# A second piece of w_out behind the experts' weights, converted in the hand-over

## The chip, the cores and the metric

The kernel runs on one core of one Trainium2 chip. The metric is the device time of one launch in microseconds (us). The engines are called PE (TensorE, matrix products), ACT (ScalarE), DVE (VectorE), POOL (GpSimd) and SP (SyncE, which here only issues transfers). SBUF is the core's working memory, PSUM the memory that PE writes to.

## The reference

Three layers follow one another on 3072 tokens of 512 features: attention in chunks with eight memory keys, a soft mixture of eight experts, and a layer with a gated normalisation. All is float32.

```python
# 1: for each chunk c of 32 queries
k_full = np.concatenate([mem_k, k_ctx], axis=2)
scores = scale * np.matmul(q_c, k_full.transpose(0, 1, 3, 2))
a = softmax(scores)
out[:, :, c_start:c_end] = np.matmul(a, v_full)
...
# 2: x is the attention's output, one row per token
logits = x @ phi
slot_input = softmax(logits, over tokens).T @ x
for e in range(E):
    h = np.maximum(slot_input[e] @ w1[e], 0.0)
    slot_out[e] = h @ w2[e]
x = softmax(logits, over slots) @ slot_out
...
# 3
h = x @ w_in
e = np.exp(h - h_max)
sm = e / (np.sum(e, axis=-1, keepdims=True) + 1e-09)
solu = h * sm
mu = np.mean(solu, axis=-1, keepdims=True)
var = np.mean((solu - mu) ** 2, axis=-1, keepdims=True)
ln = (solu - mu) / np.sqrt(var + 1e-06) * g_ln
return (ln @ w_out).astype(np.float32)
```

w_in (512x1024) and w_out (1024x512) belong to layer 3. They arrive as 64-bit words, which the kernel turns into float32 by itself; the experts' w1 and w2 arrive as float32.

## The kernel before

The program is one stream of instructions per engine, in the order in which the code is written (a manual schedule). It has four stages.

**Attention**, 0 to about 115 us: 32 steps g, each for two heads and 384 tokens. Per step SP issues the loads of keys, queries and values (`load_qk`, `load_v`) and, as the list LOADS says, one chunk of weights or none (`load_e`).

**Experts**, about 125 to 179 us: `units` lists 32 units in order, w1 or w2 of one expert and one half. Each needs two chunks of 128x1024 float32, 512 KB. Beside them run the softmax over slots (`combine`, with operations on POOL) and the conversion of w_out (`lane`).

**Hand-over**, about 179 to 197 us: the list TAIL names the steps in the order in which they are written out. `so` copies the experts' result (L491) and turns it (L495, L496); `min` multiplies it by w_in (L502) and copies the product m out in two halves (L506, L507). `ha`, `hb`, `max`, `e`, `u`, `y0`, `y1` are the first token tile's product (L595), maximum (L601), exponential (L604), product with its sum (L610) and mean taken off (L624, L628). `s0`, `t0`, `w0`, `s1`, `t1`, `w1` prepare m for the tiles behind (L514, L517, L521); `keep` is ten matmuls whose result nobody reads (L483). `yt0`, `yt1` transpose the tile on PE (L652); `hi0`, `hi1` copy that from PSUM to yh (L673, ACT), and `lo0`, `lo1` take the remainder yl (L677, DVE).

**Main stage**, to the end: 24 token tiles, each with 24 matmuls of 128x512 (L683): for each of eight pieces f of w_out, yh by whi[f], yh by wlo[f] and yl by whi[f]. `final` sorts the steps of all tiles by planned times. For tile 0 eighteen of the 24 matmuls (all of yh for pieces 0 to 6, yl for 0 to 3) stand on PE ahead of the product h(3) of tile 3 (L595), which takes the PSUM buffer that u of tile 1 (L610) has read; piece 7 of tile 0 stands behind it.

**A piece of w_out** is 128x512, one chunk of 512 KB as it arrives. Its conversion (`cast_ops`, then `wout_ops`) is a list of seven steps: two casts on ACT (L537, L538); an integer operation on DVE (L541); two more (L546, L549); the low part's product (L552) and its sum (L555), on the engine given as `eng`; whi, on ACT, with the piece's column of g as scale (L572); wlo, the remainder, on DVE (L576). w_in goes through the same `cast_ops` with its low part on POOL. In the experts' stage pieces 0 to 6 are converted on ACT and DVE. Piece 7 is converted in the hand-over: the seven steps `l` of TAIL, called `last`.

**The queue of weights.** `chunks` is the order of loading: the eight chunks of w_in and seven of w_out in turn, the 64 of the experts, then piece 7. w_in and the experts take slots from the list `free`; a piece of w_out has a slot of its own, `wslot[j]`. The slot of piece 7 is in `free` too at the start, so that it serves one experts' chunk first (`release` does not give it back). A load waits on SP for what last read its slot.

Of the kernel before, what the change touches and what calls it, by code (L numbers as in the profile page):

```python
# [7 lines left out]
FP32 = mybir.dt.float32  # L8
# [4 lines left out]
ACTF = mybir.ActivationFunctionType  # L13
ALU = mybir.AluOpType
# [42 lines left out]
TAIL = (  # L57
    "so open l l l min l l e12 ha hb max s0 s1 t0 e keep w0 u t1 y0 y1 l w1 yt0 hi0 yt1 hi1 lo0 l lo1 e3"
).split()
# [4 lines left out]
LAG = 2  # L64

CLATE = 3
TORD = [1, 0]
# [11 lines left out]
def tile_kernel(ctx: ExitStack, tc: tile.TileContext, kr, vr, w1, w2, w_in, w_out, cst, out):  # L79
# [37 lines left out]
    def at(name, off, n, dt=FP32):  # L117
        o, size, tl = arenas[name]
        assert off + n <= size, (name, off, n, size)
        v = tl[:, o + off:o + off + n]  # L120
        return v if dt == FP32 else v.bitcast(dt)
# [41 lines left out]
    wslot = [at(f"w{j}", 0, 1024) for j in range(FC)]  # L163
    free.append(wslot[-1])
    whi, wlo = {}, {}
# [32 lines left out]
    units += [("w2", E - 1, 0), ("w2", E - 1, 1)]  # L198
    chunks = [(w, j) for j in range(2 * KC) for w in ("win", "wout")][:-1]
    for u in units:  # L200
        chunks += [u[:2] + (2 * u[2] + j,) for j in range(2)]
    chunks.append(("wout", FC - 1))
    slot_of = {}
# [25 lines left out]
    def release(key):  # L229
        if slot_of[key] is not wslot[-1]:  # L230
            free.append(slot_of[key])
# [332 lines left out]

    def wout_ops(j, t):

        w = wo[t % len(wo)]

        def hi():
            area(f"w{j}", [(f"wh{j}", DM), (f"wl{j}", DM)])  # L570
            whi[j], wlo[j] = at(f"wh{j}", 0, DM, FP32R), at(f"wl{j}", 0, DM, FP32R)
            act.activation(out=whi[j], in_=w, func=ACTF.Copy, scale=g_sb[:, j:j + 1])  # L572

        return cast_ops(slot_of["wout", j], at("tmp", 512 * (t % 2), 512), w, dve) + [
            hi,
            lambda: dve.scalar_tensor_tensor(  # L576
                out=wlo[j], in0=w, scalar=g_sb[:, j:j + 1], in1=whi[j].bitcast(FP32), op0=ALU.mult, op1=ALU.subtract
            ),
        ]
# [178 lines left out]
    with tc.manual_schedule():  # L758
# [107 lines left out]
        begun = 0  # L866
        waiting = [lambda t, j=j: wout_ops(j, t) for j in range(FC - 1)]
        for n, u in enumerate(units):
# [33 lines left out]
        def e3():  # L902
# [3 lines left out]

        bufs = {}
        last = wout_ops(FC - 1, 1)
        calls = dict(
            so=m_so, open=open_final, min=m_in, l=lambda: last.pop(0)(),  # L910
        )
# [86 lines left out]
```

## Time and profile before

| | |
|---|---|
| time of the runs, median of 3 | 339.71 us (339.42 to 341.79) |
| span of the profiled execution | 340.1 us |
| busy: PE, DVE, ACT, POOL | 308.3, 248.5, 240.6, 194.3 us |
| chain that ended last, by engine | PE 57%, DMA 21%, DVE 9%, ACT 7%, POOL 3% |
| costliest group | L683 on PE, 552 matmuls, 130.5 us busy |

The profile is of one execution, and its span is compared with the median above. Times in the timelines are microseconds from the span's start. An instruction's row gives its start, its length, and in brackets how long its engine had been idle before it and for what. PE's lengths overlap, as matmuls are pipelined. The chain of waits is followed back from the last instruction, each link to what released it.

### The profile page before, as it was taken

What the parts mean: (1) busy time and instruction counts of PE and PEld (TensorE: products, weight loads), DVE (VectorE), ACT (ScalarE), POOL (GpSimd) and SP (SyncE); (2) the same over time, 40 slices, a digit from 0 to 9 for tenths busy, and PEclk for the clock granted to TensorE, in tenths of its full rate; (3) what the DMA queues carried; (4) which work ended last, traced back from release to release, by engine and by line L of the source; (5) the groups of instructions that cost most, each with busy time, mean ns of one, the idle gap of its engine ahead of it and who ended that gap; (6) DMA issues with size and microseconds to landing.
All of it is one profiled execution on the core that took longest, in us unless ns stands there. A gap on an engine that the chain in (4) does not pass through costs nothing.

```text
span 340.1 us, 8121 instructions
## 1 busy us (share of the span) xinstructions
PE 308.3 (91%) x2964; PEld 214.4 (63%) x2964; DVE 248.5 (73%) x445; ACT 240.6 (71%) x453; POOL 194.3 (57%) x381
## 2 busy tenths in 40 slices
PE   2987797898997989888989999999999999999996
PEld 1765565666665443323324778888888888888885
DVE  4787987998898338999105895887887878878540
ACT  2777958869886537685414787988888888888631
POOL 6668987797899023132100347777766667576600
PEclk9999999999999999999999999999999999999999
DMA  7999999999999999999990003566676666766621
GB/s 284 413 414 414 414 409 415 324 384 387 319 377 413 411 418 418 409 413 416 421 359 3 0 34 134 208 216 239 230 235 223 217 218 217 247 202 226 224 93 63
DMA packets 38919, 97.41 MB, mean 286 GB/s; under 512 B 4320, under 2 KB 14944, under 8 KB 38880
## 3 DMA queue, kind: packets, MB, share of 16 engines
q1 hardware_dynamic: 38736, 96.68, 75.3%
q8 instruction: 23, 0.38, 0.4%
q10 hardware_dynamic: 144, 0.22, 0.2%
q14 instruction: 16, 0.13, 0.1%
HBM read 80.11 MB, written 16.78 MB: 285 GB/s over the span
## 4 chain that ended last, share of the span: by engine, by line
PE 57%; DMA 21%; DVE 9%; ACT 7%; POOL 3%; issue 2%; SPq 0%; ACTq 0%; DVEq 0%; POOLq 0%
PE bank L683 36%; DMA e_area<-in_w_dram 9%; DMA kq_area<-in_kr_dram 7%; DMA ex_area<-in_w_dram 6%; PE h L595 3%; PE bank L303 3%; PE bank L365 2%; POOL v_area L291 2%; PE bank L243 1%; PE bank L322 1%; PE bank L314 1%; ACT s_area L275 1%; PE bank L280 1%; PE bank L328 1%; ACT s_area L317 1%
## 5 line engine op out<-in xcount | busy, mean ns | idle before, releaser
L683 PE MATMUL bank<-wh_area,yh_area 128*128 128x512 f32 x552 | 130.5, 391 | 0.0
L683 PEld LDWEIGHTS bank<-wh_area,yh_area 128*128 128x128 f32 x552 | 103.4, 188 | 22.5
L291 POOL TENSOR_SCALAR v_area<-v_area 64x780 f32<-64x780 f32 x64 | 57.0, 890 | 15.7 <-DMA v_area<-in_vr_dram 5.3
L243 PE MATMUL bank<-kq_area 128*32 128x128 f32 x768 | 29.2, 288 | 9.4 <-ACT kq_area L287 7.4
L666 DVE STREAM_TRANSPOSE yq_area<-yq_area 128x1024 f32<-128x1024 f32 x20 | 24.9, 1245 | 16.7 <-DMA yq_area<-z 16.7
L303 PE MATMUL bank<-v_area,s_area 128*32 128x130 f32 x768 | 27.9, 276 | 10.1 <-ACT s_area L283 5.7
L610 DVE SCALAR_TENSOR_TENSOR eb_area<-h,eb_area 128x1024 f32<-128x1024 f32 x24 | 29.2, 1218 | 10.5 <-ACT eb_area L604 10.1
L648 POOL TENSOR_SCALAR cst_area<-cst_area 128x1 f32<-128x1 f32 x72 | 26.8, 372 | 7.7
L243 PEld LDWEIGHTS bank<-kq_area 128*32 128x32 f32 x768 | 20.2, 114 | 15.4 <-ACT kq_area L287 9.9
L303 PEld LDWEIGHTS bank<-v_area,s_area 128*32 128x32 f32 x768 | 19.9, 108 | 15.7 <-ACT s_area L283 5.3
L601 DVE TENSOR_REDUCE cst_area<-h 128x1 f32<-128x1024 f32 x24 | 29.0, 1216 | 0.9 <-PE h L595 0.9
L637 POOL TENSOR_SCALAR cst_area<-cst_area 128x1 f32<-128x1 f32 x24 | 13.9, 579 | 25.7 <-ACT eb_area L604 23.8
L287 ACT COPY kq_area<-kq_area 64x512 f32<-64x512 f32 x39 | 23.8, 611 | 6.5 <-DMA kq_area<-in_kr_dram 6.4
L604 ACT ACTIVATE eb_area<-h,cst_area 128x1024 f32<-128x1024 f32 x24 | 26.7, 1111 | 1.9 <-DVE cst_area L601 1.9
L633 ACT ACTIVATE eb_area<-eb_area,cst_area 128x1024 f32<-128x1024 f32 x24 | 27.3, 1139 | 0.1
L630 ACT ACTIVATE eb_area<-eb_area,cst_area 128x1024 f32<-128x1024 f32 x20 | 23.1, 1155 | 5.2 <-DVE eb_area L610 4.9
L677 DVE TENSOR_TENSOR yh_area<-yq_area,yh_area 128x1024 fp32r<-128x1024 f32 x20 | 24.6, 1228 | 2.3 <-ACT yh_area L673 2.3
L673 ACT CAST yh_area<-yq_area 128x1024 fp32r<-128x1024 f32 x20 | 21.0, 1049 | 6.3 <-DVE yq_area L666 6.3
L649 POOL TENSOR_SCALAR cst_area<-cst_area 128x1 f32<-128x1 f32 x72 | 21.2, 295 | 7.1
L701 ACT ACTIVATE eb_area<-bank,cst_area 128x512 f32<-128x512 f32 x23 | 15.8, 686 | 9.2 <-POOL cst_area L639 6.9
L261 DVE TENSOR_REDUCE cst_area<-bank 128x6 f32<-128x384 f32 x32 | 17.6, 551 | 6.0 <-PE bank L243 5.9
L317 ACT COPY s_area<-bank 128x384 f32<-128x384 f32 x32 | 15.4, 483 | 7.9 <-PE bank L314 7.7
(150 smaller groups left out, 571.8 us busy)
## 6 DMA issues: line engine op xcount, KB each, us to landing
e_area<-in_w_dram SPq DMA_DIRECT2D x41, 512.0 KB, 10.1
kq_area<-in_kr_dram SPq DMA_DIRECT2D x32, 448.0 KB, 6.4
v_area<-in_vr_dram SPq DMA_DIRECT2D x32, 390.0 KB, 6.8
ex_area<-in_w_dram SPq DMA_DIRECT2D x22, 512.0 KB, 9.9
z<-eb_area SPq DMA_DIRECT2D x20, 512.0 KB, 2.8
yq_area<-z SPq DMA_DIRECT2D x80, 128.0 KB, 2.9
out_dram<-eb_area SPq DMA_DIRECT2D x23, 256.0 KB, 2.1
e_area<-in_w_in_dram SPq DMA_DIRECT2D x8, 512.0 KB, 8.1
```

The lines of the kernel that those rows point to most:

```text
L243: pe.matmul(out=bk[32 * j:32 * j + 32, t * 128:(t + 1) * 128], lhsT=kq[i][:, KS + c * CH:KS + (c + 1) * CH], rhs=kwin(g % 2, c), start=Tru ...
L287: act.copy(out=o, in_=i)
L291: pool.tensor_scalar(out=o, in0=i, scalar1=1.0, scalar2=0.0, op0=ALU.mult, op1=ALU.add)
L303: pe.matmul(out=bk[32 * j:32 * j + 32, t * 2 * VW:(t + 1) * 2 * VW], lhsT=atb[g % 2][:, c * CH:(c + 1) * CH], rhs=vz[g % 2][:, :, c * VW:( ...
L601: dve.tensor_reduce(out=sc("nm", i), in_=fin["h"][i % 2], axis=AX.X, op=ALU.max, negate=True)
L604: act.activation(out=eb[i % FIN], in_=fin["h"][i % 2], func=ACTF.Exp, bias=sc("nm", i), accum_out=sc("s", i))
L610: dve.scalar_tensor_tensor(out=ub[i % FIN], in0=fin["h"][i % 2], scalar=-1.0 / FF, in1=eb[i % FIN], op0=ALU.mult, op1=ALU.mult, accum_out= ...
L633: act.activation(out=sq, in_=ub[i % FIN], func=ACTF.Square, scale=-float(FF), bias=sc("nu", i), accum_out=sc("vs", i))
L648: pool.tensor_scalar(out=t, in0=r, scalar1=r, scalar2=xx, op0=ALU.mult, op1=ALU.mult)
L666: dve.transpose(out=yv[i % FIN].rearrange("p (f a t) -> p a f t", f=FC, a=4), in_=yq[i % FIN].rearrange("p (a f t) -> p a f t", f=FC, a=4),)
L677: dve.tensor_tensor(out=yl[i % FIN][:, sl], in0=tps(i, sl) if i < NPE else yv[i % FIN], in1=yh[i % FIN][:, sl].bitcast(FP32), op=ALU.subtract,
L683: pe.matmul(out=fin["o"][i % 2], lhsT=a[i % FIN][:, f * 128:(f + 1) * 128], rhs=w[f], start=start, stop=stop)
```

## The change

NOUT, new, is the number of pieces of w_out that are loaded ahead of the experts' weights: six instead of seven. Pieces 6 and 7 are loaded behind them, and both their slots serve an experts' chunk first. Piece 6 is no longer converted in the experts' stage: TAIL has seven new steps `p`, called `side`, that convert it in the hand-over, with its low part on POOL. Its last two steps differ from the other pieces': g is multiplied into it on POOL, ACT copies whi from that, and POOL takes wlo. Piece 7's low part moves from DVE to POOL, and its step for whi moves from ahead of `w1` to behind `hi1`. The scratch of piece 6 is the area `acc`.

```diff
 TAIL = (
-    "so open l l l min l l e12 ha hb max s0 s1 t0 e keep w0 u t1 y0 y1 l w1 yt0 hi0 yt1 hi1 lo0 l lo1 e3"
+    "so open p l p p l l min p p l l e12 ha hb max s0 s1 t0 e keep w0 u t1 y0 y1 w1 yt0 hi0 yt1 hi1 p p l lo0 l lo1 e3"
 ).split()
...
+NOUT = FC - 2
...
-    free.append(wslot[-1])
+    free += wslot[NOUT:]
...
-    chunks = [(w, j) for j in range(2 * KC) for w in ("win", "wout")][:-1]
+    chunks = [(w, j) for j in range(2 * KC) for w in ("win", "wout") if w == "win" or j < NOUT]
...
-    chunks.append(("wout", FC - 1))
+    chunks += [("wout", j) for j in range(NOUT, FC)]
...
-        if slot_of[key] is not wslot[-1]:
+        if not any(slot_of[key] is w for w in wslot[NOUT:]):
             free.append(slot_of[key])
...
-    def wout_ops(j, t):
+    def wout_ops(j, t, t2=None, eng=dve, last=None):
...
+        t2 = at("tmp", 512 * (t % 2), 512) if t2 is None else t2
+        last = last or dve
...
-            act.activation(out=whi[j], in_=w, func=ACTF.Copy, scale=g_sb[:, j:j + 1])
-
-        return cast_ops(slot_of["wout", j], at("tmp", 512 * (t % 2), 512), w, dve) + [
+            if last is pool:
+                pool.tensor_scalar(out=w, in0=w, scalar1=g_sb[:, j:j + 1], scalar2=None, op0=ALU.mult)
+                act.copy(out=whi[j], in_=w)
+            else:
+                act.activation(out=whi[j], in_=w, func=ACTF.Copy, scale=g_sb[:, j:j + 1])
+
+        if last is pool:
+            return cast_ops(slot_of["wout", j], t2, w, eng) + [
+                hi, lambda: pool.tensor_tensor(out=wlo[j], in0=w, in1=whi[j].bitcast(FP32), op=ALU.subtract),
+            ]
+        return cast_ops(slot_of["wout", j], t2, w, eng) + [
             hi,
             lambda: dve.scalar_tensor_tensor(
...
-        waiting = [lambda t, j=j: wout_ops(j, t) for j in range(FC - 1)]
+        waiting = [lambda t, j=j: wout_ops(j, t) for j in range(NOUT)]
...
-        last = wout_ops(FC - 1, 1)
+        last = wout_ops(FC - 1, 1, eng=pool)
+        side = wout_ops(FC - 2, 0, t2=acc, eng=pool, last=pool)
         calls = dict(
-            so=m_so, open=open_final, min=m_in, l=lambda: last.pop(0)(),
+            so=m_so, open=open_final, min=m_in, l=lambda: last.pop(0)(), p=lambda: side.pop(0)(),
         )
```

Line numbers behind `wout_ops` are 11 to 12 higher after the change, those ahead of it 1 higher.

On DVE, in the hand-over from the first conversion to the maximum of tile 0 and w0. First before; w7_area is piece 7 as it arrived, wo2_area its float32 form, cst_area holds scratch and small values, h0 is tile 0's product in PSUM, bank0 a PSUM bank.

```order
L541 TENSOR_SCALAR wo2_area_1800<-wo2_area_1800 128x512
L546 SCALAR_TENSOR_TENSOR wo2_area_1800<-w7_area_83,wo2_area_1800 128x512
L549 TENSOR_SCALAR cst_area_66<-wo2_area_1800 128x512
L552 TENSOR_TENSOR cst_area_66<-w7_area_83,cst_area_66 128x512
L555 TENSOR_TENSOR wo2_area_1800<-wo2_area_1800,cst_area_66 128x512
L601 TENSOR_REDUCE cst_area_66<-h0_2242 128x1
L521 SCALAR_TENSOR_TENSOR m4_area_2223<-cst_area_66,bank0_84 128x512
```

The same place after the change; w6_area is piece 6.

```order
L542 TENSOR_SCALAR wo2_area_1800<-wo2_area_1800 128x512
L547 SCALAR_TENSOR_TENSOR wo2_area_1800<-w6_area_82,wo2_area_1800 128x512
L550 TENSOR_SCALAR cst_area_66<-wo2_area_1800 128x512
L542 TENSOR_SCALAR wo2_area_1800<-wo2_area_1800 128x512
L547 SCALAR_TENSOR_TENSOR wo2_area_1800<-w7_area_83,wo2_area_1800 128x512
L550 TENSOR_SCALAR cst_area_66<-wo2_area_1800 128x512
L612 TENSOR_REDUCE cst_area_66<-h0_2232 128x1
L522 SCALAR_TENSOR_TENSOR m4_area_2213<-cst_area_66,bank0_84 128x512
```

The low part of piece 7 has left DVE, and piece 6's three integer operations stand ahead of piece 7's.

On POOL, after the change, behind the last operation of `combine` (hr_area) and ahead of tile 0's variance (the operations on one column).

```order
L433 TENSOR_TENSOR hr_area_1801<-cst_area_66,hr_area_1801 128x6x64
L553 TENSOR_TENSOR cst_area_66<-w6_area_82,cst_area_66 128x512
L556 TENSOR_TENSOR wo2_area_1800<-wo2_area_1800,cst_area_66 128x512
L553 TENSOR_TENSOR cst_area_66<-w7_area_83,cst_area_66 128x512
L556 TENSOR_TENSOR wo2_area_1800<-wo2_area_1800,cst_area_66 128x512
L576 TENSOR_SCALAR wo2_area_1800<-wo2_area_1800,cst_area_66 128x512
L583 TENSOR_TENSOR wh6_area_2293<-wo2_area_1800,wh6_area_2293 128x512
L648 TENSOR_SCALAR cst_area_66<-cst_area_66 128x1
```

All six operations on 128x512 are new there; before, the first operation on one column (L637) followed `combine` directly.

On ACT, from t1 to the square of tile 0 (the last row). First before; h1 is the second PSUM buffer of the tiles' product, t and bank1 hold the transposed tile, wh7_area is whi[7].

```order
L517 CAST cst_area_66<-h1_2243 128x512
L628 ACTIVATE eb_area_2262<-eb_area_2262,cst_area_66 128x4x4x32
L572 ACTIVATE wh7_area_2285<-wo2_area_1800,cst_area_66 128x512
L673 CAST yh_area_2261<-bank1_85 128x512
L673 CAST yh_area_2261<-t_2241 128x512
L633 ACTIVATE eb_area_2262,cst_area_66<-eb_area_2262,cst_area_66 128x1024
```

The same place after.

```order
L518 CAST cst_area_66<-h1_2233 128x512
L639 ACTIVATE eb_area_2259<-eb_area_2259,cst_area_66 128x4x4x32
L684 CAST yh_area_2258<-bank1_85 128x512
L684 CAST yh_area_2258<-t_2231 128x512
L577 CAST wh6_area_2293<-wo2_area_1800 128x512
L579 ACTIVATE wh7_area_2297<-wo2_area_1800,cst_area_66 128x512
L644 ACTIVATE eb_area_2259,cst_area_66<-eb_area_2259,cst_area_66 128x1024
```

whi[7] has moved behind the two casts to yh, and whi[6] stands ahead of it. On DVE the rows behind are unchanged in order: yl, wlo[7], yl, and the maxima of tiles 1 and 2.

## Rows read from the trace of the kernel before

**Rows 1.** The chain of waits, 130 to 230 us: start, length, engine and line.

```profile
165.62 10.12 DMA e_area<-in_w_dram
175.78 1.05 PE bank L475 x4
...
195.23 1.24 DVE eb_area L610 x2
...
217.12 5.49 PE bank L683 x24
```

**Rows 2.** The stages table: busy time by engine, PE's granted clock, DMA share, GB/s.

```profile
160.00:175.00 15.00, 14.19 (x88) 4.31 (x82) 2.61 (x10) 6.07 (x16) 1.52 (x2) 1.00 1.03 418
```

**Rows 3.** The timeline of ACT in the hand-over: start, length, instruction, idle time before it.

```profile
179.93 0.68 ACT L537 ACTIVATE wo_area<-w_area 128x512 f32<-128x512 f32 x1
180.50 0.65 ACT L538 ACTIVATE w_area<-w_area 128x512 f32<-128x512 uint32 x1
182.48 0.59 ACT L506 COPY hr_area<-bank 128x512 f32<-128x512 f32 x1 [1.32 <-PE bank L502]
...
189.64 0.71 ACT L572 ACTIVATE wh_area<-wo_area,cst_area 128x512 fp32r<-128x512 f32 x1
190.26 0.58 ACT L673 CAST yh_area<-bank 128x512 fp32r<-128x512 f32 x1
190.73 0.59 ACT L673 CAST yh_area<-t 128x512 fp32r<-128x512 f32 x1
191.21 1.17 ACT L633 ACTIVATE eb_area<-eb_area,cst_area 128x1024 f32<-128x1024 f32 x1
```

**Rows 4.** The timeline of DVE in the hand-over.

```profile
181.15 0.42 DVE L541 TENSOR_SCALAR wo_area<-wo_area 128x512 int32<-128x512 int32 x1
181.60 0.69 DVE L546 SCALAR_TENSOR_TENSOR wo_area<-w_area,wo_area 128x512 int32<-128x512 int32 x1
182.33 0.43 DVE L549 TENSOR_SCALAR cst_area<-wo_area 128x512 int32<-128x512 int32 x1
...
185.16 1.23 DVE L601 TENSOR_REDUCE cst_area<-h 128x1 f32<-128x1024 f32 x1 [0.89 <-PE h L595]
...
190.87 0.69 DVE L677 TENSOR_TENSOR yh_area<-bank,yh_area 128x512 fp32r<-128x512 f32 x1 [0.71 <-ACT yh_area L673]
191.48 0.74 DVE L576 SCALAR_TENSOR_TENSOR wh_area<-wo_area,cst_area,wh_area 128x512 fp32r<-128x512 f32 x1
...
192.74 2.35 DVE L601 TENSOR_REDUCE cst_area<-h 128x1 f32<-128x1024 f32 x2
```

**Rows 5.** The timeline of PE in the hand-over.

```profile
189.56 0.66 PE L652 MATMUL bank<-cst_area,eb_area 128*128 128x128 f32 x4 [0.38 <-DVE eb_area L624]
...
191.41 4.29 PE L683 MATMUL bank<-wh_area,yh_area 128*128 128x512 f32 x18
196.51 0.73 PE L595 MATMUL h<-m_area,c4t_area 128*128 128x512 f32 x2 [0.81 <-DVE eb_area L610]
```

**Rows 6.** The load of w_out's piece 7: its issue, and how long until it landed.

```profile
169.35 0.33 SPq L225 DMA_DIRECT2D w_area<-in_w_out_dram  x1
...
DMA to landing us min/median/max: 10.2/10.2/10.2
```

**Rows 7.** POOL's groups for w_in's low parts: count, busy us, mean ns, idle before.

```profile
L552 POOL TENSOR_TENSOR cst_area<-e_area,cst_area 128x512 f32<-128x512 f32 x8 | 10.6, 1320 | 0.7
L555 POOL TENSOR_TENSOR cst_area<-cst_area 128x512 f32<-128x512 f32 x8 | 10.3, 1289 | 0.7
```

**Rows 8.** Timelines of POOL and DVE, two moments at which both work on SBUF.

```profile
98.84 1.86 POOL L291 TENSOR_SCALAR v_area<-v_area 64x780 f32<-64x780 f32 x2
100.02 0.95 DVE L541 TENSOR_SCALAR cst_area<-cst_area 128x512 int32<-128x512 int32 x1
...
146.37 1.01 POOL L432 TENSOR_TENSOR hr_area<-cst_area,hr_area 128x384 fp32r<-128x384 f32 x1 [3.67 <-ACT hr_area L428]
146.48 1.44 DVE L546 SCALAR_TENSOR_TENSOR wo_area<-w_area,wo_area 128x512 int32<-128x512 int32 x1
```

## Prediction

> **What bounds the kernel now.** I read the chain of waits first, then the stages table for the stretch where the chain is made of transfers, then the timelines of ScalarE (ACT), VectorE (DVE) and TensorE (PE) in the hand-over, and last the grouped rows of GpSimd (POOL).
>
> The chain [rows 1] shows three stretches around the change. From about 126 us until 175.74 it is one transfer of experts' weights behind another; the last such hop is shown, and PE's work on that chunk starts 0.04 us after the landing. (It is the third-last chunk; the last two land 1.25 us apart under the work that follows.) Then comes the hand-over, 175.8 to 196.5 us: short links of PE, ACT and DVE, none of them long. Behind 196.5 us the chain is PE alone, main matmuls (L683) to the end. So a microsecond saved or lost anywhere in the first two stretches arrives at the end of the program, as long as nothing beside the chain catches up.
>
> In the stages table [rows 2] the DMA engines are full from 160 to 175 us (share 1.03) at 418 GB/s. A chunk is 512 KB, 524,288 bytes, so one chunk takes 524288 / 418e3 = 1.25 us. That is the price of one place in the queue. In the same stretch PE, which waits for each chunk, shows a granted clock of 1.00, the 2.4 GHz level.
>
> In the hand-over every microsecond has an owner. ACT [rows 3] converts w_out piece 7 (L537, L538) between the copies of the slots' result and those of m_in, and makes whi[7] (L572) at 189.64, ahead of the two yh casts, which start at 190.26 and 190.73. That L572 is hidden: yh's first half could not start earlier, since the four transposes before it end at 189.56 + 0.66 = 190.22 [rows 5]. DVE [rows 4] converts piece 7 from 181.15 on (three integer operations, then the two of the low part), then has 0.89 us of idle time before max(0) at 185.16; later it runs yl, wlo[7] (191.48), yl, max(1) and max(2) (192.74) without a gap. PE sits idle 0.81 us [rows 5] for DVE's L610 at 195.23, the u of tile 1. DVE is therefore what sets the start of the main stage.
>
> **What the change does to the queue.** Piece 6 of w_out leaves the places in front of the experts' weights and goes behind them; its slot takes an experts' chunk instead, once. The attention loads and the number of chunks issued between them stay. Before, the last experts' chunk is the 79th of the weights' chunks (8 w_in, 7 w_out, 64 experts'); after, the 78th. The ring is one slot longer, so every place in the queue waits for the same release as before: the first chunk in the extra area is the 33rd place in both, the first one in a reused slot the 44th in both. The queue has work without a gap over this stretch, so the last experts' chunk lands one place earlier: **-1.25 us** [rows 2].
>
> The two pieces behind it are not late. Piece 7 was issued at 169.35 and landed 10.2 us later, at 179.55 [rows 6], three places behind the chunk of 175.74 (175.74 + 3 x 1.25 = 179.5); its place does not move, and piece 6 comes one place ahead of it, at about 178.3. ACT asks for piece 6 at 179.93 - 1.25 = 178.68 and for piece 7 two operations later (0.57 apart, [rows 3]) at 179.82. The cover is 0.3 us for either.
>
> **What the change does to the hand-over.** All times from here are on the clock of before; the shift of -1.25 us is added at the end.
>
> ACT: four conversions instead of two, 179.93 + 4 x 0.57 = 182.2, the last ending near 182.3. The copy of m_in's first half starts at 182.48 [rows 3], for PE. Hidden, by 0.2 us. ACT also loses the conversions of piece 6 in the experts' stage, and DVE its six operations there; that stage waits for transfers, so I count nothing.
>
> DVE before max(0): six operations (the integer parts of pieces 6 and 7) instead of five. The lengths of a triple are 0.42, 0.69 and 0.43 [rows 4]. Alone, the second triple would run 182.7 to 184.3, and max(0) would not notice. But now POOL works beside it: the four low-part operations, 1.32 and 1.29 us each [rows 7], the first as soon as piece 6's triple ends at 182.76.
>
> Here the trace has a warning [rows 8]. L546, 0.69 us at 181.60, took 1.44 us when it was issued at 146.48 behind a POOL operation that ran 146.37 to 147.38; it ended 0.54 us behind POOL. L541, 0.42 us at 181.15, took 0.95 at 100.02, with two POOL operations from 98.84 to 100.70; it ended 0.27 us behind them. So these DVE operations, which read and write only SBUF, stand still until POOL's has ended, and then need their length less about 0.15. Working this through: the first operation of piece 7 gets in before POOL (182.7 to 183.1); POOL's first holds until about 184.2; the DVE operation issued at 183.13 ends at 184.2 + 0.54 = 184.74; POOL's second, queued behind it, holds until about 185.85; DVE's last, short one ends at about 185.85 + 0.27 = 186.12, and max(0) starts at 186.05 instead of 185.16: **+0.9 us**. Bounds: 0, if they do not meet, since the idle 0.89 us covers the rest; 1.3, if POOL takes its second turn before DVE gets one (both DVE operations then follow 185.5: 0.54 + 0.43, max(0) near 186.45). I take 0.9, as in rows 8 DVE was let in when a POOL operation ended.
>
> The Trainium skill, page "SBUF — State Buffer", section "Who interferes with whom", has the same meeting as an exclusive lock: the second to issue blocks fully until the first is done. Read literally, DVE's whole length would follow POOL's end, 0.69 rather than 0.54, which over three blocked operations adds some 0.45 us to my sum below, 341.3 us in place of 340.8. The 0.54 us behind POOL in [rows 8] speaks for the shorter form.
>
> POOL itself is not late: its third and fourth operation end near 188.8, the multiplication by g at 190.1 at most (at the price of a two-input one, 1.32), and ACT wants it at 192.1 (below).
>
> DVE before max(1): whi[7] now stands on ACT behind both yh casts and the new cast whi[6]. ACT issues these 0.48 apart [rows 3], so whi[6] takes the place of L633 at 191.21 and whi[7] runs 191.69 to 192.40 (0.71). DVE's wlo[7], which stands between the two yl, ran at 191.48; it now starts at 192.43: **+0.95 us**. The second yl, max(1), max(2) and u(1) stand behind it on DVE, and PE's h(3) behind u(1). Nothing on DVE hides this, as there was no gap after 190.87. L633 and its variance on POOL move back by 1.0 to 1.5 us too; tile 0 needs its scale only when its matmuls are done, several us later.
>
> POOL's last new operation, wlo[6], starts when whi[6] is done, 0.6 us before wlo[7] is issued on DVE (0.48, and 0.12 that whi[7] is longer). It holds 1.3 us. wlo[7] has two SBUF inputs, so it stands 0.7 us and then needs some 0.57 instead of 0.74: **+0.53 us**. Bounds: 0 without a meeting, 0.7 with its whole length behind.
>
> PE does not mind: of the 18 main matmuls that stand before h(3) [rows 5] the last two use piece 6, at about 191.41 + 16 x 0.23 = 195.1 (195.1 + 0.9 with max(0) late). wlo[6] is done at about 192.7 + 1.3 = 194.0 on that count. Piece 7 comes behind h(3).
>
> **Sum.** -1.25 + 0.9 + 0.95 + 0.53 = +1.13 us. The profiled execution spans 340.1 us; 341.2 after. The median of the runs is 339.71, 0.4 below the profiled one, so 340.8. A measurement of this kernel tells about 1% (3.4 us) from no change, so this counts as no change.
>
> **Rivals.**
> *The engines do not meet.* The POOL operations fall into DVE's gaps, and only the late whi[7] costs: -1.25 + 0.95 = -0.3, 339.4 us. For it: the idle 0.89 us. Against it: rows 8, and that POOL's first operation starts on the very end of DVE's. Chance 0.17.
> *The gain arrives whole.* wlo[7] is not held up, as ACT starts yh and whi[7] sooner than I say: -1.25, 338.5 us. Against it: the first yh cast waits for transposes, and the order on ACT is fixed. Chance 0.08.
> *More is lost.* Both bounds above, 1.3 and 0.7: -1.25 + 1.3 + 0.95 + 0.7 = +1.7, 341.4 us, or another half microsecond if the last piece of w_out lands late by more than its 0.3 us of cover. Chance 0.09.
> *The clock falls.* This is the one that would be slower by over 1%. PE's gap before h(3) grows from 0.81 us [rows 5] by the 0.95 and the 0.53 to 2.3 us (the 0.9 falls ahead of its 18 matmuls). If PE is granted 1.2 GHz after it and stays there for one tile, 24 main matmuls, 5.49 us at 2.4 GHz [rows 1], take 5.5 us more: +6.6, 346.3 us. It decides once the lower level lasts for 10 matmuls (10 x 0.23 = 2.3 us, and 1.1 of the sum: 1%). Against it: with PE waiting for each chunk from 160 to 175 us the granted clock was 1.00 [rows 2]. Chance 0.04.
> My forecast, 340.8, with its own range 340.3 to 341.5: 0.62.
>
> **How the numbers follow.** Leaving out the whole gain and the fallen clock (0.12) and a little spread of the runs at either end, the range is 338.8 to 341.8. Faster by over 1% would need more than the whole gain: 0.02. Slower by over 1%: the clock, 0.04. Within 1%: 0.94.
>
> **What the profile after should show.** The chain's last transfer ends at about 174.5. On DVE, the integer operations of piece 7 last 1.0 us and more where they took 0.69 and 0.43, and no idle time is left before max(0); wlo[7] waits for ACT and lasts about 1.2 us; PE's idle time before h(3) is over 2 us, and h(3) starts near 197.6. Wrong, if DVE's operations keep their lengths beside POOL, if max(0) still waits for PE, or if that transfer ends at the old time.

## The result and the profile after

The changed kernel is slower. Its median is 343.12 us (eight runs, 341.20 to 344.79) beside 340.40 us for the kernel before (eight runs, 339.42 to 341.79): a ratio of 1.0086, 95% interval 1.0065 to 1.0108, or +2.9 us where +1.1 was forecast. A second set of runs gave 1.0103 (1.0086 to 1.0120), +3.5 us. The forecast time, 340.8, and the top of its range, 341.8, both lie below the median. One run of 501.9 us (POOL's low parts exchanged) and one of 600.9 us (the hand-over alone) lie far off all others and are left out below.

The profiled execution spans 340.9 us at a granted clock of 1.00; the one before spanned 340.1. The runs' own list gives for each run a span. The time lies above it by 1.8 to 2.0 us in the kernel before (mean 1.90 of 76 later runs) and by 1.9 to 2.2 in the changed one (mean 2.10 of 14), so 0.2 us of the loss lie outside the span, where no trace shows what they are. The middle span of the later runs of before is 337.9 (26 runs), 2.2 us shorter than the profiled one. So the two profiled spans are not subtracted here. I compare the stretch in which the change lies: from PE's first matmul on the chain's last transfer to h(3), the product of tile 3. Behind h(3) the two profiled executions are alike: 340.1 − 196.5 and 340.9 − 197.4, 143.6 and 143.5 us.

The chain of waits of the kernel after (start, length, engine and line; lines here are one higher than before in the first part of the code, eleven to twelve higher behind `wout_ops`):

```profile
163.52 10.08 DMA e_area<-in_w_dram
...
173.64 1.05 PE bank L476 x4
...
181.02 1.68 DVE wo_area L547
...
184.02 1.22 DVE cst_area L612
...
187.82 0.96 DVE eb_area L635
...
191.84 1.22 DVE wh_area L587
...
196.06 1.24 DVE eb_area L621 x2
...
197.35 0.73 PE h L606 x2
```

The stretch lasts 197.35 − 173.64 = 23.71 us; in [rows 1, 5] it lasted 196.51 − 175.78 = 20.73. It is 2.98 us longer, and four rows of DVE that were not on the chain, or were short on it, hold the difference. DVE's timeline after:

```profile
180.57 0.42 DVE L542 TENSOR_SCALAR wo_area<-wo_area 128x512 int32<-128x512 int32 x1
181.02 1.67 DVE L547 SCALAR_TENSOR_TENSOR wo_area<-w_area,wo_area 128x512 int32<-128x512 int32 x1
182.72 1.38 DVE L550 TENSOR_SCALAR cst_area<-wo_area 128x512 int32<-128x512 int32 x1
184.02 1.21 DVE L612 TENSOR_REDUCE cst_area<-h 128x1 f32<-128x1024 f32 x1
185.15 0.73 DVE L522 SCALAR_TENSOR_TENSOR m_area<-cst_area,bank 128x512 fp32r<-128x512 f32 x1
...
187.82 0.95 DVE L635 TENSOR_SCALAR eb_area<-eb_area,cst_area 128x512 f32<-128x512 f32 x1
...
190.14 0.69 DVE L688 TENSOR_TENSOR yh_area<-bank,yh_area 128x512 fp32r<-128x512 f32 x1 [0.72 <-ACT yh_area L684]
191.84 1.22 DVE L587 SCALAR_TENSOR_TENSOR wh_area<-wo_area,cst_area,wh_area 128x512 fp32r<-128x512 f32 x1 [1.01 <-ACT wh_area L579]
```

POOL's timeline beside it:

```profile
180.78 1.35 POOL L553 TENSOR_TENSOR cst_area<-w_area,cst_area 128x512 f32<-128x512 f32 x1 [19.93 <-DVE cst_area L550]
182.21 1.60 POOL L556 TENSOR_TENSOR wo_area<-wo_area,cst_area 128x512 f32<-128x512 f32 x1
184.23 1.31 POOL L553 TENSOR_TENSOR cst_area<-w_area,cst_area 128x512 f32<-128x512 f32 x1 [0.42 <-issue]
185.62 1.29 POOL L556 TENSOR_TENSOR wo_area<-wo_area,cst_area 128x512 f32<-128x512 f32 x1
186.91 1.58 POOL L576 TENSOR_SCALAR wo_area<-wo_area,cst_area 128x512 f32<-128x512 f32 x1
191.20 1.31 POOL L583 TENSOR_TENSOR wh_area<-wo_area,wh_area 128x512 fp32r<-128x512 f32 x1 [2.71 <-ACT wh_area L577]
```

ACT's, at the copy of m_in's first half and behind the transposes:

```profile
180.37 0.59 ACT L507 COPY hr_area<-bank 128x512 f32<-128x512 f32 x1
...
190.48 0.64 ACT L577 CAST wh_area<-wo_area 128x512 fp32r<-128x512 f32 x1
191.00 0.73 ACT L579 ACTIVATE wh_area<-wo_area,cst_area 128x512 fp32r<-128x512 f32 x1
```

Read the three together, each time against the start of the stretch, with [rows 4] for before:

| step on DVE | before | after | added here |
|---|---|---|---|
| max(0) starts (L601, now L612) | 9.38 | 10.38 | +1.00 |
| first yl starts (L677, now L688) | 15.09 | 16.50 | +0.41 |
| wlo[7] starts (L576, now L587) | 15.70 | 18.20 | +1.09 |
| h(3) on PE | 20.73 | 23.71 | +0.48 |

max(0) has lost its 0.89 us of idle time, as L547 and L550 stood still beside POOL's first two operations. y0 (L635) took 0.95 us and not 0.49 beside POOL's multiplication by g. wlo[7] waits 1.01 us for whi[7], which now stands on ACT behind both casts to yh and whi[6]. And wlo[7] itself takes 1.22 us and not 0.74, beside POOL's wlo[6]. PE, last, waits for all of them:

```profile
188.83 0.66 PE L663 MATMUL bank<-cst_area,eb_area 128*128 128x128 f32 x4 [1.77 <-DVE eb_area L635]
...
190.69 4.24 PE L694 MATMUL bank<-wh_area,yh_area 128*128 128x512 f32 x18
197.35 0.73 PE L606 MATMUL h<-m_area,c4t_area 128*128 128x512 f32 x2 [2.42 <-DVE eb_area L621]
...
198.15 1.09 PE L663 MATMUL t<-cst_area,eb_area 128*128 128x128 f32 x8
199.00 1.40 PE L694 MATMUL bank<-wh_area,yh_area 128*128 128x512 f32 x5
...
200.69 3.61 PE L694 MATMUL bank<-wh_area,yh_area 128*128 128x512 f32 x15
```

With the queue's 1.2 us off, 2.98 is +1.8 us, and the runs say +2.9 and +3.5. The profiled execution does not hold the rest, but the list of runs does: five of the eight have a mean granted clock of 0.994 or 0.995, the other three of 0.998 or 1.00. Of the 73 runs of the kernel before in the first three sets of experiments (26, 30 and 17) none lies below 0.998. That was the rival "the clock falls", and the experiments had to say whether it is the cause and what it costs.

### The profile page after: what moved, and what is told of

It is laid out like the page before. It is cut to its first block, busy times and chain, and to the rows that moved or that the text cites. A ratio compares the mean times of both kernels' runs of the same rounds, so it can differ in the third digit from the quotient of the medians.

```text
span 340.9 us, 8120 instructions
## 1 busy us (share of the span) xinstructions
PE 308.5 (90%) x2964; PEld 214.3 (63%) x2964; DVE 247.3 (73%) x440; ACT 240.7 (71%) x453; POOL 200.1 (59%) x387
## 4 chain that ended last, share of the span: by engine, by line
PE 50%; DMA 14%; DVE 6%; ACT 4%; issue 1%; POOL 0%; DVEq 0%; SPq 0%; ACTq 0%
PE bank L694 36%; DMA e_area<-in_w_dram 8%; DMA ex_area<-in_w_dram 6%; PE h L606 3%; PE bank L304 2%; PE bank L366 1%; PE bank L323 1%; PE bank L315 1%; PE bank L704 1%; PE t L704 1%; PE t L663 1%; DVE eb_area L621 1%; PE bank L476 1%; PE bank L329 1%; ACT eb_area L615 1%
## 5 line engine op out<-in xcount | busy, mean ns | idle before, releaser
L677 DVE STREAM_TRANSPOSE yq_area<-yq_area 128x1024 f32<-128x1024 f32 x20 | 24.9, 1245 | 19.4 <-DMA yq_area<-z 19.4
L660 POOL TENSOR_SCALAR cst_area<-cst_area 128x1 f32<-128x1 f32 x72 | 25.1, 349 | 7.1
L659 POOL TENSOR_SCALAR cst_area<-cst_area 128x1 f32<-128x1 f32 x72 | 24.6, 341 | 7.6
L612 DVE TENSOR_REDUCE cst_area<-h 128x1 f32<-128x1024 f32 x24 | 28.9, 1213 | 0.0
L688 DVE TENSOR_TENSOR yh_area<-yq_area,yh_area 128x1024 fp32r<-128x1024 f32 x20 | 24.6, 1232 | 2.3 <-ACT yh_area L684 2.3
L276 ACT ACTIVATE s_area<-s_area 128x384 f32<-128x384 f32 x32 | 16.9, 529 | 3.0 <-DVE s_area L267 2.8
```

The costliest lines, as they stand in the source:

```text
L612: dve.tensor_reduce(out=sc("nm", i), in_=fin["h"][i % 2], axis=AX.X, op=ALU.max, negate=True)
L659: pool.tensor_scalar(out=t, in0=r, scalar1=r, scalar2=xx, op0=ALU.mult, op1=ALU.mult)
L660: pool.tensor_scalar(out=r, in0=t, scalar1=1.5, scalar2=r, op0=ALU.add, op1=ALU.mult)
L677: dve.transpose(out=yv[i % FIN].rearrange("p (f a t) -> p a f t", f=FC, a=4), in_=yq[i % FIN].rearrange("p (a f t) -> p a f t", f=FC, a=4),)
L688: dve.tensor_tensor(out=yl[i % FIN][:, sl], in0=tps(i, sl) if i < NPE else yv[i % FIN], in1=yh[i % FIN][:, sl].bitcast(FP32), op=ALU.subtract,
```

## Experiments

The theories were these. **Waits and meetings**: the hand-over lost what the table above says, the queue gave its place back, and nothing else happened. **The clock**: the wait of 2.4 us before h(3) lets PE's clock fall, and that costs something on top. Beside them, that the queue's gain never came, as the late pieces spoil something else.

### The changed kernel again

> The changed kernel once more, for its spans and granted clocks beside those of the kernel before. If the loss lies only in the hand-over's engines (theory 1), the runs of both kernels have the same mean granted clock, and the spans differ by about -1.25 + 3.0 = +1.7 us: 20.77 us from the landing at 175.74 to h(3) at 196.51 before, 23.75 from 173.60 to 197.35 after. If the clock falls in the longer idle time of PE (theory 2), the runs of the changed kernel split: those with a mean clock near 0.995 are about 1.7 us longer than those near 1.000 (3.4 us at half rate in 341 us), and the runs of the kernel before stay near 1.000.

Measured: 343.42 us (six runs) against 339.85 (26 runs), ratio 1.0103 (1.0086 to 1.0120). All six runs have a granted clock of 0.993 to 0.995, and this time the profiled execution is one of them. PE's timeline of this run:

```profile
196.68 0.73 PE L606 MATMUL h<-m_area,c4t_area 128*128 128x512 f32 x2 [2.36 <-DVE eb_area L621]
...
197.49 1.50 PE L663 MATMUL t<-cst_area,eb_area 128*128 128x128 f32 x8
198.63 2.48 PE L694 MATMUL bank<-wh_area,yh_area 128*128 128x512 f32 x5
200.91 0.87 PE L606 MATMUL h<-m_area,c4t_area 128*128 128x512 f32 x2
201.62 4.51 PE L694 MATMUL bank<-wh_area,yh_area 128*128 128x512 f32 x19
```

Its stages table (columns as in [rows 2]) ahead of the long rows, over them and behind them:

```profile
196.00:198.00 2.00, 1.32 (x8) 1.01 (x9) 1.96 (x4) 1.79 (x4) 0.70 (x3) 1.00 0.00 0
198.00:201.50 3.50, 3.50 (x13) 2.92 (x12) 2.54 (x4) 1.30 (x2) 1.23 (x3) 0.51 0.02 5
201.50:210.00 8.50, 8.50 (x43) 7.07 (x42) 6.64 (x8) 6.82 (x11) 5.19 (x18) 1.00 0.09 34
```

The granted clock is still 1.00 right behind PE's idle time, 0.51 on the mean from 198.0 to 201.5 us, and 1.00 again behind that. At the 1.2 GHz level it would be 0.50, so the level lasted about 0.49 x 3.50 / 0.50 = 3.4 us. The five main matmuls took 2.48 us where they took 1.40, the eight transposes 1.50 where 1.09. From h(3) to the run of main matmuls of the next tile it is 201.62 − 196.68 = 4.94 us, in the execution without a fall 200.69 − 197.35 = 3.34, with no idle time of PE in either. The fall costs **1.6 us**.

The hand-over itself was 196.68 − 173.45 = 23.23 us here, 0.48 shorter than in the first profile: y0 took its 0.49 us this time, and it was POOL's multiplication that took longer. DVE's row:

```profile
187.63 0.49 DVE L635 TENSOR_SCALAR eb_area<-eb_area,cst_area 128x512 f32<-128x512 f32 x1
```

and POOL's:

```profile
186.71 1.86 POOL L576 TENSOR_SCALAR wo_area<-wo_area,cst_area 128x512 f32<-128x512 f32 x1
```

POOL's row starts 0.92 us ahead of DVE's here and 0.91 in the first profile, so the starts do not show what decides which of the two is held. That half microsecond is lost in some executions and not in others.

### The queue alone

The queue of the changed kernel with the hand-over of the kernel before. Piece 6 is loaded but not converted; piece 5 stands in for it.

```diff
-    "so open p l p p l l min p p l l e12 ... w0 u t1 y0 y1 w1 yt0 hi0 yt1 hi1 p p l lo0 l lo1 e3"
+    "so open l l l min l l e12 ... w0 u t1 y0 y1 l w1 yt0 hi0 yt1 hi1 lo0 l lo1 e3"
...
-        last = wout_ops(FC - 1, 1, eng=pool)
-        side = wout_ops(FC - 2, 0, t2=acc, eng=pool, last=pool)
+        last = wout_ops(FC - 1, 1)
+        side = []
+        whi[FC - 2], wlo[FC - 2] = whi[FC - 3], wlo[FC - 3]
```

> Only the queue's part of the change: piece 6 is loaded behind the experts' weights, its slot serves an experts' chunk, and the hand-over is that of before (piece 7 alone, low part on DVE). Piece 6 is not converted at all; the matmuls that would use it use piece 5 a second time. If one place in the queue is worth 1.25 us and the hand-over is the whole loss: 1.25 us faster than before, and 20.8 us from the landing to h(3). Rival, the queue is worth nothing, as the attention stage or a slot sets the transfers: no change. Rival, the reordered queue itself is what loses: slower than before.

Measured: 338.75 us against 339.85, ratio 0.9964 (0.9950 to 0.9977), −1.2 us. PE's row, with the 0.81 us of [rows 5] back:

```profile
192.77 0.73 PE L606 MATMUL h<-m_area,c4t_area 128*128 128x512 f32 x2 [0.81 <-DVE eb_area L621]
```

The hand-over is 192.77 − 172.00 = 20.77 us, as before. The place in the queue is worth what was forecast, and the pieces that arrive behind it spoil nothing.

### whi[7] back in its old place

```diff
-  ... y0 y1 w1 yt0 hi0 yt1 hi1 p p l lo0 l lo1 e3
+  ... y0 y1 l w1 yt0 hi0 yt1 hi1 p p lo0 l lo1 e3
```

> The changed kernel with one step put back: whi[7] ahead of w1, where it was before. If wlo[7] waiting for it on DVE is a term of its own, max(1) comes 0.95 + 0.5 us earlier (the meeting with wlo[6] on POOL goes too): 1.5 us faster than the changed kernel, still about 0.3 slower than before. Rival, the maximum's delay and the meetings with POOL make up all of it: less than 0.5 us faster than the changed kernel. With PE's idle time before h(3) cut from 2.4 to about 1 us, theory 2 also expects a mean clock of 1.000 in all runs.

Measured: 340.05 us against 339.85, ratio 1.0004 (0.9991 to 1.0016). No clock below 0.998 in twelve runs. ACT's timeline shows whi[7] ahead of the casts to yh, DVE's shows wlo[7] neither waiting nor held:

```profile
187.12 0.71 ACT L579 ACTIVATE wh_area<-wo_area,cst_area 128x512 fp32r<-128x512 f32 x1
188.18 0.59 ACT L684 CAST yh_area<-bank 128x512 fp32r<-128x512 f32 x1 [0.35 <-PE bank L663]
```

```profile
189.41 0.74 DVE L587 SCALAR_TENSOR_TENSOR wh_area<-wo_area,cst_area,wh_area 128x512 fp32r<-128x512 f32 x1
```

The first cast still waits 0.35 us for PE behind whi[7], so the old place cost nothing. This one `l` took out the wait (1.09), the meeting (0.48) and the fall of the clock: the hand-over is 194.44 − 172.32 = 22.12 us, 1.59 less than in the first profile of after, and the time is 3.4 us less than that of the same set.

### Piece 7's triple ahead of POOL's work

POOL's two low parts change places. Piece 7's, which waits for the end of its three integer operations (the triple) on DVE, comes first.

```diff
-  so open p l p p l l min p p l l e12 ...
+  so open p l p p l l min l l p p e12 ...
```

> The changed kernel with POOL's two low parts exchanged: piece 7's first, which waits for the last integer operation on DVE, then piece 6's. So no operation of POOL runs beside the integer operations, and max(0) should wait for PE again, as before: 1.0 us earlier than in the changed kernel. But POOL's four operations then last until about 189.5 on the clock of before and meet y0 on DVE (0.49 us at 189.02), which gives some of it back: 0.3 to 1.0 us faster than the changed kernel. If DVE's delay before max(0) does not come from meeting POOL, nothing changes.

Measured: 342.08 us (eleven runs) against 339.85, ratio 1.0050 (1.0030 to 1.0070). DVE's timeline:

```profile
179.83 0.69 DVE L547 SCALAR_TENSOR_TENSOR wo_area<-w_area,wo_area 128x512 int32<-128x512 int32 x1
180.56 0.43 DVE L550 TENSOR_SCALAR cst_area<-wo_area 128x512 int32<-128x512 int32 x1
181.87 1.22 DVE L612 TENSOR_REDUCE cst_area<-h 128x1 f32<-128x1024 f32 x1 [0.89 <-PE h L606]
```

Both operations have their lengths back, and max(0) its 0.89 us of idle time. The hand-over is 195.25 − 172.45 = 22.80, 0.91 less than after. PE still waits before h(3):

```profile
195.25 0.73 PE L606 MATMUL h<-m_area,c4t_area 128*128 128x512 f32 x2 [2.41 <-DVE eb_area L621]
```

Five of eleven runs have a clock of 0.993 to 0.995: their median is 342.47, that of the six others 340.58, 1.9 us apart. The same difference is 2.4 us within the changed kernel (five runs against three) and 1.0 within the kernel with the earlier gap filled (four against three, below). With so few runs in each group, these agree with the 1.6 us of the trace only roughly.

### Matmuls that nobody reads in PE's gap before h(3)

```diff
             put(b + TO, emit_out, n)
+        put(HS[3] - 0.01, keep_clock, fin["o"][1], 9)
```

> The changed kernel with nine more matmuls whose result nobody reads, on PE between the 18 main matmuls of tile 0 and h(3), into a free PSUM bank: 9 x 0.22 = 1.9 us of the 2.4 us in which PE waits there. They change no other engine's work. If PE's idle time before h(3) lets the clock fall (theory 2), no run has a mean clock near 0.994 any more, and the median is 1.6 us below the changed kernel's. If the clock falls for the earlier idle time (1.3 to 1.8 us before tile 0's transposes) or for something else, the falls stay, and the median stays or rises.

Measured: 341.56 us against 339.63, ratio 1.0051 (1.0035 to 1.0067). No clock below 0.999 in twelve runs. PE's timeline:

```profile
193.32 2.26 PE L484 MATMUL bank<-wh_area,c4t_area 128*128 128x512 f32 x9
195.86 0.73 PE L606 MATMUL h<-m_area,c4t_area 128*128 128x512 f32 x2 [0.28 <-DVE eb_area L621]
```

The hand-over is as long as after's (195.86 − 172.16 = 23.70), DVE is as late, but PE works through the gap, and the clock stays up. What is left, +1.7 us, is the waits and meetings less the queue: 2.97 − 1.2. This tells the two theories apart: both are true, and the clock's part is the difference to +2.9 and +3.5.

### The same matmuls in the earlier gap

PE has a second gap after the change, 1.77 us before the transposes. Six more matmuls of `keep` fill that one.

```diff
-KEEP = (0, 2, 0, 10)
+KEEP = (0, 2, 0, 16)
```

> The changed kernel with the ten matmuls that nobody reads made sixteen: 1.3 us more of PE's idle time before tile 0's transposes is filled, and the idle time before h(3) stays. If the later gap is the one that counts, the falls stay in most runs and the median is that of the changed kernel. If the earlier one counts, they are gone and the median is 1.6 us lower.

Measured: 343.00 us against 339.63, ratio 1.0089 (1.0058 to 1.0120); four of seven runs at 0.993 to 0.995. PE's timeline and the stages table of the profiled execution:

```profile
187.60 0.66 PE L663 MATMUL bank<-cst_area,eb_area 128*128 128x128 f32 x4 [0.36 <-DVE eb_area L635]
...
196.11 1.08 PE L606 MATMUL h<-m_area,c4t_area 128*128 128x512 f32 x2 [2.36 <-DVE eb_area L621]
```

```profile
196.00:200.00 4.00, 3.89 (x14) 3.35 (x15) 2.71 (x6) 1.88 (x3) 1.49 (x4) 0.57 0.00 0
```

The earlier gap is down to 0.36 us, and the clock falls all the same behind the later one. With the later one filled, it stayed up beside an earlier gap of 1.76 us. So it is the gap before h(3) that counts. From h(3) to the run of main matmuls of the next tile it is 201.02 − 196.11 = 4.91 us here, again 1.6 more than without a fall.

### Both moves, and a version with less on POOL

The first is whi[7] early together with the triple ahead of POOL:

> The changed kernel with both steps put right: whi[7] ahead of w1, and POOL's low parts exchanged so that none runs beside DVE's integer operations. If the two terms add (1.6 and 0.9 us of hand-over, from 23.7 to 22.1 and to 22.8), the hand-over takes 21.2 us from the landing to h(3) and the clock stays up: 0.8 us faster than before, 339.1 us. What would be left over before's 20.7 is y0 on DVE, which takes 0.95 instead of 0.49 us beside POOL. If the terms overlap: 339.6 to 340.

Measured: 339.37 us against 339.63, ratio 0.9983 (0.9965 to 1.0001); hand-over 193.13 − 171.90 = 21.23; no clock below 0.999. What is left over the old 20.73 is y0, which took 0.96 us from 185.17, beside POOL's last low-part sum (L556, 184.56 to 185.85): as POOL starts later here, y0 meets this one and not the multiplication. The second takes that away too: the product of piece 7's low part goes back to DVE, where it fits into the idle time ahead of max(0), so that POOL is done as y0 starts, and the multiplication by g goes to ACT.

```diff
-  so open p l p p l l min p p l l e12 ... y0 y1 w1 yt0 hi0 yt1 hi1 p p l lo0 l lo1 e3
+  so open p l p p l l l min l p p e12 ... y0 y1 l w1 yt0 hi0 yt1 hi1 p p lo0 l lo1 e3
...
-            eng.tensor_tensor(out=dst, in0=dst, in1=t2, op=ALU.add)
+            (end or eng).tensor_tensor(out=dst, in0=dst, in1=t2, op=ALU.add)
...
-                pool.tensor_scalar(out=w, in0=w, scalar1=g_sb[:, j:j + 1], scalar2=None, op0=ALU.mult)
+                act.activation(out=w, in_=w, func=ACTF.Copy, scale=g_sb[:, j:j + 1])
...
-        last = wout_ops(FC - 1, 1, eng=pool)
+        last = wout_ops(FC - 1, 1, end=pool)
```

> As the last one, but POOL is kept off DVE altogether: the product of piece 7's low part goes back to DVE, its sum and piece 6's two low operations on POOL come behind it and end before y0, the multiplication by g goes to ACT behind yh, whi[7] stands ahead of w1. If meetings with POOL and the late whi[7] are the whole loss, the hand-over takes 20.8 us again, y0 takes 0.49, and the whole gain of the queue arrives: 338.7 us, 1.1 to 1.25 faster than before, as in the kernel that changes only the queue. If something else in the change costs (the loads at the end, ACT's four conversions), it is slower than that.

> The kernel that keeps POOL off DVE once more, as its first comparison left 0.2 to 1.4 us of gain open. If its hand-over is that of before (20.8 us) and the queue gives its 1.2 us, it is 0.8 to 1.4 us faster than before, 338.5 to 339. If something of the gain is lost that the one profile did not show, 0.5 us or less.

Measured: 339.15 us against 339.63, ratio 0.9976 (0.9958 to 0.9993), and in the second set 339.14 against 340.21, 0.9976 (0.9959 to 0.9994). DVE's timeline of the first:

```profile
181.08 0.69 DVE L553 TENSOR_TENSOR cst_area<-w_area,cst_area 128x512 f32<-128x512 f32 x1
181.86 1.22 DVE L612 TENSOR_REDUCE cst_area<-h 128x1 f32<-128x1024 f32 x1
...
185.71 0.49 DVE L635 TENSOR_SCALAR eb_area<-eb_area,cst_area 128x512 f32<-128x512 f32 x1
```

and POOL's:

```profile
181.85 1.26 POOL L556 TENSOR_TENSOR wo_area<-wo_area,cst_area 128x512 f32<-128x512 f32 x1 [21.07 <-DVE cst_area L553]
...
184.46 1.29 POOL L556 TENSOR_TENSOR wo_area<-wo_area,cst_area 128x512 f32<-128x512 f32 x1
```

While POOL works, 181.85 to 185.75, DVE has only operations that read PSUM (max, w0, u); y0 starts as POOL ends. The hand-over is 193.21 − 172.43 = 20.78 us, as before the change. This version is 0.8 us faster than the kernel before and some 4 us faster than the change as made. That is less than the 1.1 to 1.25 expected at first, and the interval reaches from −0.2 to −1.4. The list of runs tells where the difference lies. The mean span is 1.0 us shorter than before's in the first set (336.96 beside 337.99) and 1.2 in the second (337.11 beside 338.34), so within the span the queue's gain arrives. But the time of a run lies 2.26 us above its span here (24 runs) and 1.90 before. The other 0.4 us is outside the span, and what it is stays open.

### The hand-over alone

The other half of the change: piece 6 in its old place in the queue, converted as the change does.

```diff
+NFRONT = FC - 1
...
-    free += wslot[NOUT:]
+    free += wslot[NFRONT:]
...
-    chunks += [("wout", j) for j in range(NOUT, FC)]
+    chunks += [("wout", j) for j in range(NFRONT, FC)]
```

> Only the hand-over's part of the change: piece 6 is loaded where it was before, ahead of the experts' weights, but converted in the hand-over with POOL as in the changed kernel. If the two parts add, the hand-over takes 23.7 us from the landing to h(3) as in the changed kernel, against 20.7 before, and the queue gives nothing: 3.0 us slower than before with the clock up, 4.6 in a run in which it falls (1.6 us), so 343 to 344.5 us. If the hand-over was slow because pieces 6 and 7 land late, the early piece 6 makes it faster than 23.7 us.

> The hand-over's part alone once more, for a profile in which PE runs at its usual rate throughout. If the parts add, h(3) starts 23.7 us behind the first matmul after the chain's last transfer, as in the changed kernel; if pieces 6 and 7 landing late was part of the loss, it starts earlier.

Measured: 344.21 us (five runs) against 340.21, ratio 1.0119 (1.0093 to 1.0144), with four of the five runs at 0.994 or 0.995. A second measurement of the same kernel, of two runs, gave 1.0144 (1.0072 to 1.0216) and the profile:

```profile
196.54 1.22 PE L607 MATMUL h<-m_area,c4t_area 128*128 128x512 f32 x2 [2.42 <-DVE eb_area L622]
```

The hand-over is 196.54 − 173.32 = 23.22 us, as in the second profile of the changed kernel (23.23): y0 took its 0.49 us in both. An early piece 6 helps nothing. The loss is all in the hand-over.

## Why the prediction was wrong, and where it was right

One sum comes within 0.6 us of all the kernels: the hand-over's length over 20.73 us, less 1.2 us where the queue is changed, plus 1.6 us for the share of runs in which the clock fell.

| kernel | hand-over | queue | clock | sum | measured (95%) |
|---|---|---|---|---|---|
| changed | +2.98 | −1.2 | 5 of 8: +1.0 | +2.8 | +2.9 (2.2 to 3.7) |
| changed, again | +2.50 | −1.2 | 6 of 6: +1.6 | +2.9 | +3.5 (2.9 to 4.1) |
| queue alone | +0.04 | −1.2 | none | −1.2 | −1.2 (−1.7 to −0.8) |
| whi[7] early | +1.39 | −1.2 | none | +0.2 | +0.1 (−0.3 to +0.5) |
| triple first | +2.07 | −1.2 | 5 of 11: +0.7 | +1.6 | +1.7 (1.0 to 2.4) |
| later gap filled | +2.97 | −1.2 | none | +1.8 | +1.7 (1.2 to 2.3) |
| earlier gap filled | +2.96 | −1.2 | 4 of 7: +0.9 | +2.7 | +3.0 (2.0 to 4.1) |
| both moves | +0.50 | −1.2 | none | −0.7 | −0.6 (−1.2 to 0.0) |
| less on POOL | +0.05 | −1.2 | none | −1.2 | −0.8 (−1.4 to −0.2) |
| hand-over alone | +2.49 | 0 | 4 of 5: +1.3 | +3.8 | +4.0 (3.2 to 4.9) |

(Measured is the ratio's excess times the median of before in the same set. The queue's −1.2 is itself the third row's result, so that row checks only the hand-over. The hand-over alone takes its length from the second measurement. The time outside the span is not in the sum: with its 0.2 us "changed, again" comes to +3.1, with the 0.4 of "less on POOL" that row comes to −0.8.)

Of the 1.8 us between the forecast +1.1 and the measured +2.9, the fall of the clock holds 1.0. The hand-over holds 0.6, as it grew by 2.98 us where terms B, C and D below together forecast 2.38. The time outside the span holds 0.2.

**The rival of the clock: the step that failed.** The prediction reckoned that PE's gap before h(3) would grow to 2.3 us; it was 2.42. It then gave a fall of the clock 0.04, and for that it used the wrong row. [rows 2] shows a clock of 1.00 "with PE waiting for each chunk", but in that same row PE is busy 14.19 of 15 us: its waits there are short, and the row says nothing of an idle stretch of 2.3. No row of before has such a stretch shortly ahead of full work at a known clock: behind the first microseconds, the longest idle stretch of PE in that trace is 1.57 us, ahead of its matmuls at 27.24, and the granted clock from 20 to 40 us is 1.00. So the rival stood without evidence either way, and 0.04 was a choice, not a reading. Its price was wrong too, in the other direction: it put the low level at a whole tile, 11 us for a cost of 5.5, and the trace shows 3.4 us of it for a cost of 1.6. At that price the rival gives 340.8 + 1.6 = 342.4, inside 1% but outside the range. The two mistakes leave one lesson: a rival with an unknown length should have entered the range from its small end.

**B, max(0): right.** +0.9 was forecast, +1.00 came, and by the steps told: L547 got held by POOL's first operation, POOL's second waited for it and held L550 in turn. The sum's form, the length less about 0.15 behind POOL's end, held: L547 ended at 182.69, 0.56 behind POOL's 182.13, and L550 at 184.10, 0.29 behind 183.81. The Trainium skill, page "SBUF — State Buffer", section "Who interferes with whom", says that the second to issue is blocked fully until the first is done. These rows agree that it stands still; but read literally the whole length, 0.69 and 0.43, would follow POOL's end, and the rows show less.

**C, the wait for whi[7]: right in kind, slightly small.** +0.95 was forecast, +1.09 came.

**D, wlo[7] beside wlo[6]: right.** +0.53 was forecast, +0.48 came (1.22 us for 0.74; it ended 0.55 behind POOL's end at 192.51).

**Missing: y0 beside the multiplication by g.** The prediction's own times showed it: POOL's multiplication from 188.8 to 190.1, and y0, which the timeline of before has at 189.02, some 0.9 late with max(0), so at 189.9, inside it. The multiplication then took 1.58 us where 1.32 was taken, which made the overlap longer. The prediction asked only whether ACT waits for POOL, not whom POOL holds on the way. The price is some 0.45 us (0.95 for 0.49, +0.41 in the table of the hand-over), in those executions in which it is y0 that is held.

**A, the queue: right**, −1.25 forecast and −1.2 measured (the queue alone). That ACT's two more conversions are hidden was right as well: the copy of m_in's first half came 6.73 us into the stretch, and 6.70 before.

**The base.** "0.4 below the profiled one" compared a span with the times of runs, which lie about 1.9 us above their spans. The forecast was made from the median, so this moved nothing; it did hide that the profiled execution was 2.2 us longer than the middle one of the later runs.

**The signs in the profile** came: both integer operations over 1 us, no idle time before max(0), wlo[7] at 1.22 us, PE's idle time 2.42. That h(3) started at 197.35, where 197.6 was written, is luck: the chain's last transfer ended at 173.60, 0.9 us ahead of the 174.5 written, and the hand-over was 0.6 us longer than forecast. A reader of the one profile would have called the forecast right. The fall of the clock lies in executions that it does not show.

**Left open:** why the same gap is followed by a fall in one run and by none in the next (2.42 us and 1.00 in the first profile; 2.36 and 0.51 in the second). The Trainium skill, page "TensorE: Matmul & The Clock Gate", section "Part 1: The HAM clock gate (the "warmup" mystery)", says that the chip's watch over PE's activity runs on by itself and is not set back when a program starts, so that the point of a change of clock varies from run to run. That would fit the different starts of the low level told at the end, and it is not tested here.

## What to carry to other kernels

Price a gap of the matrix engine not only at its length: look how long the gap is against the longest one that the trace shows with the clock still up (here 2.4 us against 1.57), and if it is longer, take a fallen clock into the range. When work goes to POOL, list for each of its operations which DVE operations on SBUF alone lie in the same microseconds, all the way down and not only at the place that was moved, and put beside it those that read PSUM. Before moving an operation behind others on its engine, ask who waits for its result. whi[7] cost nothing in its old place, where ACT would have waited for PE without it.

## What the hardware showed that was not expected

With 2.36 to 2.42 us without a matmul before h(3), PE's granted clock fell to the 1.2 GHz level in 5 of 8 and 6 of 6 runs of the changed kernel, 5 of 11 with the triple first, 4 of 7 with the earlier gap filled, and 6 of 7 of the hand-over alone. With that gap at 0.28 to 0.85 us it fell in none of 69 runs of five kernels, although two of these (whi[7] early, later gap filled) kept 1.74 and 1.76 us of idle time before the transposes. (The gaps are those of the profiled executions.) In both stages tables shown the low level lasted 3.4 us (0.43 x 4.00 / 0.50 in the second). But it began within h(3) where the earlier gap was filled, and h(3) took 1.08 us; in the changed kernel it began 1.3 us behind the start of h(3), which took its usual 0.73.

Which engine is held is not settled by the order of the program alone: of y0 and POOL's multiplication by g, DVE was held in one execution of the changed kernel (0.95 us for 0.49) and POOL in another (1.86 us for 1.58), with starts 0.91 and 0.92 us apart in the profile.
